# Later maskings, a later range check and another staging tile in a three-stage attention kernel

## The chip, the cores and the metric

The kernel runs on one core of one Trainium2 chip. The metric is the device time of one execution in microseconds (us). All runs compared here are of the fast state; executions of one kernel scatter: 45 of the kernel before, on one chip, lay between 2189.8 and 2222.5 us, with a median of 2202.0.

## The reference, cut to what matters

The output is a gated sum of two attention branches over 2048 tokens of width 640.

```
g = sigmoid((x * gate_w).sum(-1))
a = sliding-window attention, 32 heads of 20, window 256        # A_ref
b = recurrence over 64 segments of 32 tokens, each with 8       # B_ref
    memory tokens made from the segment before, 32 heads of 192
out = g * a + (1 - g) * b
```

## The kernel before

It has three stages. The **sliding branch** takes the tokens in 16 blocks of 128. The **tail** is named after the last 8 of each segment's 32 tokens: it computes their projections for all segments at once, before the recurrence. The **recurrent branch** follows, three quarters of the time.

In the sliding branch a group of scores goes through TensorE (scores), ScalarE (exponential) and VectorE (masking by a minimum), and its values are multiplied two groups later. Between these, "filling units" make the projections of the next block; they share two banks (tag "p") of PSUM, the memory that matmuls write to, and VectorE or ScalarE copies them out:

```python
def probs(qb, hf, u, pr):
    ...                                             # 8 score matmuls
    nc.scalar.activation(out=pt, in_=sp[:], func=ACT.Exp, scale=scale)
    ...
    nc.vector.tensor_tensor(out=pt, in0=pt, in1=pat..., op=ALU.min)      # the masking
...
for i, (hf, u, pr, done) in enumerate(units):
    (probs_exact if exact else probs)(qb, hf, u, pr)
    while fill and spent * total < (i + 1) * time:  # filling units
        w, f = fill.pop(0); f(); spent += w
    ready.append([(qb, hf, g, pr) for g in done])
    if len(ready) > 2:
        for v in ready.pop(0): values(*v)           # two groups later
if exact or qb == NB - 1 or len(chunks(qb + 1)) != nk:
    ...                                             # empties ready
```

The tail's loop, over four groups g of 24 units (eight banks "ps"):

```python
tail.qk(g, *u, tps, "ps")
if i == 11:
    tail.store_qk(g, 0)
    if g == 0:
        ... omg_sb memset and loads ...             # GpSimd
        step_c = step_constants(tc, bconst, chk)    # GpSimd; VectorE's mk_x inside
...
if g == 0 and i == 14:
    range_flag(tc, chk, tps, rl_all, flag)          # VectorE's check, then a count matmul
```

`step_constants` ends with `mk_x`, a VectorE reduction of `mk_h`, which GpSimd makes. The tail's query and key units are staged in two tiles, `holds[0]` for the first half of the segments, `holds[1]` for the second; the values that follow are staged in `holds[1]`.

## Time and profile before

In the lines of the profile PE is TensorE, PEld its weight loads, DVE VectorE, ACT ScalarE, POOL GpSimd, SP SyncE; L241 is line 241 of that run's kernel. A line of the order in time has start and duration in us, and in brackets the engine's idle time before it and what ended that. The granted clock is the share of full speed at which TensorE's clock ran.

| before | us |
|---|---|
| median of the first 3 runs | 2198.5 |
| profiled execution | 2206.7 |
| its sliding branch, to the store of the last gate column | 316.8 |
| its tail, to the first recurrent projection | 174.5 |
| its recurrent branch | 1715.4 |
| TensorE's granted clock, mean | 0.977 |

The stage marks are the start of the write of omg_dram (316.81 us) and of the first ps_k matmul (491.31 us). The lines of the waits and of the order in time stand in the prediction. The row of the page that shows the clock, in tenths of full speed over 40 slices of 55 us, before:

```profile
PEclk9998988999999999999999999999999999999999
```

The first two eights are in the sliding branch, the third (331 to 386 us) is in the tail. How it looks at 1 us, in a table of windows (busy time of PE, PEld, DVE, ACT and POOL, each with its number of instructions, then clock, DMA share and GB/s):

```profile
102.00:103.00 1.00, 0.67 (x19) 0.58 (x16) 0.62 (x2) 1.00 (x2) 0.00 (x0) 1.00 0.02 5
103.00:104.00 1.00, 0.21 (x4) 0.21 (x4) 1.00 (x3) 1.00 (x2) 0.00 (x0) 1.00 0.93 248
104.00:105.00 1.00, 1.00 (x26) 0.87 (x23) 0.97 (x4) 0.24 (x1) 0.13 (x1) 1.00 0.80 304
105.00:106.00 1.00, 1.00 (x18) 0.97 (x19) 1.00 (x2) 0.98 (x1) 1.00 (x4) 0.61 0.09 16
```

TensorE pauses for 1.1 us of two, and at 105 us its clock falls to half, for 13.7 us. Summed over such windows from 30 us to its end, the sliding branch loses 23.9 us of clock (one minus the granted clock, times time). That is no loss of run time as it stands: TensorE isn't the limit all the time.

### The profile page before, as it was taken

How to read it: one execution, taken by the hardware profiler on the slowest of the kernel's cores; microseconds unless marked ns; L12 is line 12 of the kernel's file. 1: busy time of each engine (PE TensorE's matmuls, PEld its weight loads, DVE VectorE, ACT ScalarE, POOL GpSimd, SP SyncE). 2: the span in 40 equal slices, each digit the busy share in tenths (PEclk: the TensorE clock that was granted, in tenths of full speed). 3: DMA queues.
4: the chain of work that ended last, by engine and by line, in shares of the span. 5: the costliest groups of instructions: out<-in, count | busy, mean ns of one | idle time of the engine just before them, and what ended most of it. 6: DMA issues, size and time to landing. Idle time of an engine off the chain costs nothing. (4 is left out here: it accounts for less than half of the span.)

```text
span 2206.7 us, 92693 instructions
## 1 busy us (share of the span) xinstructions
PE 1959.8 (89%) x39670; PEld 1455.9 (66%) x39670; DVE 1032.0 (47%) x3338; ACT 914.2 (41%) x1885; POOL 717.8 (33%) x2011
## 2 busy tenths in 40 slices
PE   7889988998988889989998898899988899898897
PEld 6777767756666666666666666666666666666665
DVE  5777753234444444444444444444444444444444
ACT  4766742233443434434433333344334343333343
POOL 4111102133333333333333333333333333333332
PEclk9998988999999999999999999999999999999999
DMA  4222119579999999999999999999999999999998
GB/s 140 75 69 71 43 26 320 140 213 344 362 352 346 340 349 355 360 347 348 364 347 336 351 356 342 342 356 360 348 344 356 354 356 350 362 337 355 336 352 287
DMA packets 278374, 655.81 MB, mean 297 GB/s; under 512 B 42552, under 2 KB 62144, under 8 KB 277952
## 3 DMA queue, kind: packets, MB, share of 16 engines
q1 hardware_dynamic: 246464, 602.01, 76.0%
q0 software_dynamic: 31488, 47.78, 7.5%
q8 instruction: 313, 5.13, 0.9%
q14 instruction: 109, 0.89, 0.1%
HBM read 620.26 MB, written 29.37 MB: 294 GB/s over the span
## 5 line engine op out<-in xcount | busy, mean ns | idle before, releaser
L763 PEld LDWEIGHTS <-b_hT 128*32 128x32 bf16 x15360 | 377.5, 96 | 311.4 <-issue 114.3
L954 PEld LDWEIGHTS <-b_OT 128*64 128x64 bf16 x6144 | 400.9, 110 | 67.2 <-issue 59.4
L954 PE MATMUL ps_o<-b_w,b_OT 128*64 128x320 bf16 x2560 | 300.4, 302 | 36.9 <-DMA b_w<-in_B_Wo_dram 33.0
L774 ACT CAST b_tok<-ps_k 128x384 bf16<-128x384 f32 x256 | 122.7, 479 | 441.3 <-PE ps_k L763 441.2
L763 PE MATMUL ps_k<-w_k,b_hT 128*32 128x384 bf16 x4096 | 246.8, 329 | 19.0 <-DVE b_hT L980 18.7
L954 PE MATMUL ps_o<-hold,b_OT 128*64 128x320 bf16 x2560 | 238.7, 302 | 0.0
L763 PE MATMUL ps_v<-w_v,b_hT 128*32 128x384 bf16 x3840 | 229.0, 328 | 7.2 <-issue 6.8
L763 PE MATMUL ps_q<-w_q,b_hT 128*32 128x384 bf16 x3840 | 235.2, 329 | 0.0
L239 ACT ACTIVATE pt<-s_ps 128x1024 bf16<-128x1024 f32 x180 | 180.7, 1024 | 75.3 <-PE s_ps L236 73.1
L934 ACT CAST b_OT<-ps_pv 128x480 bf16<-128x480 f32 x256 | 143.2, 559 | 164.7 <-PE ps_pv L930 114.0
L810 DVE COPY b_K<-tr_k 128x256 bf16<-128x256 bf16 x256 | 73.4, 287 | 291.3 <-PE tr_k L787 286.3
L774 ACT CAST b_vtok<-ps_v 128x384 bf16<-128x384 f32 x256 | 122.9, 480 | 168.2 <-PE ps_v L763 167.8
L963 DVE CAST b_osum<-ps_o 128x320 bf16<-128x320 f32 x64 | 31.5, 492 | 338.4 <-PE ps_o L954 338.4
L774 ACT CAST b_tok<-ps_q 128x384 bf16<-128x384 f32 x256 | 122.7, 479 | 112.5 <-PE ps_q L763 111.2
L716 POOL DMA_DIRECT2D b_xg<-xin x256 | 139.4, 545 | 84.9 <-POOL b_QT L800 57.0
L241 DVE TENSOR_TENSOR pt<-pt,pat 128x1024 bf16<-128x1024 bf16 x180 | 126.7, 708 | 69.6 <-ACT pt L239 69.4
L787 PEld LDWEIGHTS <-b_tok 128*64 128x64 bf16 x3072 | 100.6, 110 | 82.8 <-issue 33.5
L852 DVE TENSOR_REDUCE sm<-S_ps 128x4 f32<-128x160 f32 x256 | 82.1, 321 | 156.3 <-PE S_ps L841 149.1
L985 POOL DMA_DIRECT2D b_dram<-b_osum x128 | 64.2, 506 | 265.1 <-DVE b_osum L963 256.7
L986 POOL DMA_DIRECT2D b_ga<-ga_dram x128 | 63.5, 497 | 265.1 <-DMA out_dram<-b_ga 259.9
L907 DVE TENSOR_TENSOR b_PTm<-PT_ps,mk_m 128x320 bf16<-128x320 f32 x256 | 123.7, 483 | 49.2 <-PE PT_ps L895 47.2
L819 POOL COPY b_K<-b_xg 128x64 bf16<-128x64 bf16 x256 | 61.4, 240 | 258.8 <-PE S_ps L841 130.6
(142 smaller groups left out, 3832.4 us busy)
## 6 DMA issues: line engine op xcount, KB each, us to landing
b_w<-in_B_Wo_dram SPq DMA_DIRECT2D x640, 320.0 KB, 5.3
b_w<-in_B_Wq_dram SPq DMA_DIRECT2D x320, 384.0 KB, 5.6
b_w<-in_B_Wv_dram SPq DMA_DIRECT2D x320, 384.0 KB, 5.5
b_w<-in_B_Wk_dram SPq DMA_DIRECT2D x256, 384.0 KB, 5.7
xin<-hold POOLq DMA_DIRECT2D x8, 1536.0 KB, 9.7
b_xg<-xin POOLq DMA_DIRECT2D x256, 48.0 KB, 4.9
w_k<-in_B_Wk_dram SPq DMA_DIRECT2D x16, 384.0 KB, 3.3
b_xv<-xin POOLq DMA_DIRECT2D x64, 96.0 KB, 5.7
```

Of the source, the lines that this page charges most:

```text
L239: nc.scalar.activation(out=pt, in_=sp[:], func=ACT.Exp, scale=scale)
L241: nc.vector.tensor_tensor(out=pt, in0=pt, in1=pat.unsqueeze(1).to_broadcast([P, 2, 512]), op=ALU.min)
L716: sc.op("DMA", 500, lambda: nc.gpsimd.dma_start(tile_of(b)[:].rearrange("p i b t -> p (i b t)"), xin[s, :, c:c + 192]), writes=[b])
L763: nc.tensor.matmul(t[32 * j:32 * j + 32, 0:384], lhsT=tile_of(hT)[:, kt, :], rhs=w[:, j * 384:(j + 1) * 384], start=(kt == 0), stop=(kt == ...
L774: nc.scalar.copy(dst, src)
L787: nc.tensor.transpose(t[64 * a:64 * a + 64, k, :], tok["tile"][:, c:c + 64], ident[:], tile_position=(0, 64 * a))
L810: nc.vector.tensor_copy(tile_of(K02)[:, :, :, 0:SEG], src)
L852: nc.vector.tensor_reduce(out=x["mx"][:], in_=view(), axis=AX.X, op=ALU.max)
L907: nc.vector.tensor_tensor(out=tile_of(PTm)[:], in0=src.to_broadcast([P, 2, 4, L]), in1=mk_m[:].unsqueeze(1).unsqueeze(3).to_broadcast([P, ...
L934: sc.op("ACT", act(480), lambda: nc.scalar.copy(tile_of(OT)[:, 0:12 * L], o["tile"][:, 0:12 * L]), reads=[o], writes=[OT])
L954: nc.tensor.matmul(t[64 * h:64 * h + 64, 0:D // 2], lhsT=OT["tile"][:, c:c + 64], rhs=w, start=(g == 0 and m == 0 and n == 0), stop=(g == ...
L985: sc.op("DMA", 500, lambda h=h: nc.gpsimd.dma_start(half(b_dram, h), mine(osum["tile"], h)), reads=[osum])
```

## The change

Its intent: VectorE should not stand before an instruction that cannot start while others behind it could, and a staging tile should not be reused while its store is on the way. Nothing is computed differently.

```diff
-            nc.vector.tensor_tensor(out=pt, in0=pt, in1=pat..., op=ALU.min)
+            return lambda: nc.vector.tensor_tensor(out=pt, in0=pt, in1=pat..., op=ALU.min)
 ...
-                q0, q4, k4 = ([(140, lambda: dense.pop(0)(ps_p, "p"))] for _ in range(3))
+                q0, k0, q4 = ([(140, lambda: dense.pop(0)(ps_p, "p"))] for _ in range(3))
 ...
-                (probs_exact if exact else probs)(qb, hf, u, pr)
+                cut_next = (probs_exact if exact else probs)(qb, hf, u, pr)
+                if cut is not None:
+                    cut()
+                cut = cut_next
 ...
             if exact or qb == NB - 1 or len(chunks(qb + 1)) != nk:
+                if cut is not None:
+                    cut()
+                    cut = None
 ... tail: step_constants ahead of omg_sb, mk_x as c.last, the count as a function
-                    if g == 0 and i == 14:
-                        range_flag(tc, chk, tps, rl_all, flag)
+                    if g == 0 and i == 12:
+                        count = range_flag(tc, chk, rl_all, flag)
+                    if g == 1 and i == 0:
+                        step_c.last()
+                        count(tps, "ps")
 ... tail values
-        slot = self.holds[1][:, tt * PIECE:(tt + 1) * PIECE]...
+        slot = self.holds[0][:, tt * PIECE:(tt + 1) * PIECE]...
-                    if g == 0 and tt == 1:
+                    if g == 0 and tt == 3:
-                            weights.load_held(holds[0], i, u, nc.sync)
+                            weights.load_held(holds[1], i, u, nc.sync)
```

More of the change, by code (lines that the diff above doesn't have):

```diff
@@ L240, in probs @@
             pat = pats[nk][:].rearrange("p g c q -> p (g c) q")[:, 4 * u:4 * u + 4, :].rearrange("p i q -> p (i q)")
-            nc.vector.tensor_tensor(out=pt, in0=pt, in1=pat.unsqueeze(1).to_broadcast([P, 2, 512]), op=ALU.min)
+            return lambda: nc.vector.tensor_tensor(out=pt, in0=pt, in1=pat.unsqueeze(1).to_broadcast([P, 2, 512]), op=ALU.min)
         def probs_exact(qb, hf, u, pr):
@@ L300, in branch_A @@
         spread(1)
-        ready = []
+        ready, cut = [], None
         for qb in range(NB):
@@ L364, in mix, with range_flag @@
             nc.sync.dma_start(outf[rows, :], ga[:])
-def range_flag(tc, const, psum, rl_all, flag):
+def range_flag(tc, const, rl_all, flag):
     nc = tc.nc
@@ L378, in range_flag, with count @@
     nc.vector.memset(ones[:], 1.0)
-    n = psum.tile([1, 1], FP32, name="n_ok", tag="ps")
-    nc.tensor.matmul(n[:], lhsT=both[:], rhs=ones[:], start=True, stop=True)
-    nc.vector.tensor_scalar(out=flag[:], in0=n[:], scalar1=127.5, scalar2=None, op0=ALU.is_lt)
+    def count(psum, tag):
+        n = psum.tile([1, 1], FP32, name="n_ok", tag=tag)
+        nc.tensor.matmul(n[:], lhsT=both[:], rhs=ones[:], start=True, stop=True)
+        nc.vector.tensor_scalar(out=flag[:], in0=n[:], scalar1=127.5, scalar2=None, op0=ALU.is_lt)
+    return count
 L = MEM + SEG
@@ L586, in v @@
     def v(self, g, tt, pool, tag):
-        slot = self.holds[1][:, tt * PIECE:(tt + 1) * PIECE].rearrange("p (j c) -> p j c", j=4)
+        slot = self.holds[0][:, tt * PIECE:(tt + 1) * PIECE].rearrange("p (j c) -> p j c", j=4)
         xv = self.xin[:, :, KT * SEG + 768:XIN]
@@ L649, in step_constants @@
     mk_x = const.tile([P, 4], FP32, name="mk_x")
-    nc.vector.tensor_reduce(out=mk_x[:], in_=mk_h[:].rearrange("p g j -> p j g"), axis=AX.X, op=ALU.add)
     mk_z = const.tile([P, 2], FP32, name="mk_z")
@@ L656, in step_constants @@
     c = Constants()
+    c.last = lambda: nc.vector.tensor_reduce(out=mk_x[:], in_=mk_h[:].rearrange("p g j -> p j g"), axis=AX.X, op=ALU.add)
     c.still, c.ident, c.mask, c.mk_m, c.mk_x, c.mk_z = still, ident, mask, mk_m, mk_x, mk_z
@@ L1118 @@
                         if g == 0:
+                            step_c = step_constants(tc, bconst, chk)
                             nc.gpsimd.memset(omg_sb[:], 0.0)
@@ L1122 @@
                                     nc.gpsimd.dma_start(omg_sb[64 * h + MEM:64 * h + L, :], omg_dram[:].rearrange("(s t) -> t s", t=SEG))
-                            step_c = step_constants(tc, bconst, chk)
                         tail.fetch("q", g + 1)
                         tail.fetch("k", g + 1)
-                    if g == 0 and i == 14:
-                        range_flag(tc, chk, tps, rl_all, flag)
+                    if g == 0 and i == 12:
[3 more added lines that the diff above has]
+                        count(tps, "ps")
                         nc.gpsimd.dma_start(flag_dram[:], flag[:])
@@ L1140 @@
                     tail.v(g, tt, tps, "ps")
-                    if g == 0 and tt == 1:
+                    if g == 0 and tt == 3:
                         for i, u in enumerate(last[:HOLD]):
-                            weights.load_held(holds[0], i, u, nc.sync)
+                            weights.load_held(holds[1], i, u, nc.sync)
     with ExitStack() as bctx:
-        branch_B(bctx, tc, xin, mem0, weights, ring, step_c, omg_sb, ga_dram, b_dram, outf, holds[1], last[HOLD:])
+        branch_B(bctx, tc, xin, mem0, weights, ring, step_c, omg_sb, ga_dram, b_dram, outf, holds[0], last[HOLD:])
     wctx.close()
```

## The prediction

> **What bounds the kernel now.** I first read the table of busy shares (TensorE 89% of 2206.7 us, every other engine under 50%), then the slices in time, then tables of busy time over short windows, the list of waits of TensorE, and the instructions in order of time where it stood still. The program has three stages: the sliding branch to about 311 us, the tail (memory tokens' projections) to 490 us, the recurrent branch to the end. The change touches only the first two, so only TensorE's idle time and slow-clock time before 490 us can be won; the other 1717 us run the same instructions in the same order.
>
> The list of waits of TensorE, sliding branch without its start (30 to 311 us):
> ```profile
> PE qk_ps L138 <- DVE QT_blk L144: 11.9, 14, 1.0
> PE qk_ps L138 <- DVE KT_blk L144: 10.9, 13, 1.5
> PE s_ps L236 <- ACT pt L239: 3.1, 14, 0.5
> PE aT_ps L198 <- DVE an L291: 3.0, 2, 2.1
> PE o_ps L280 <- DVE pt L241: 1.1, 2, 0.6
> ```
> The columns are total us, times, longest us. Two waits a block of 128 tokens, near 0.9 us each, are for a projection bank that VectorE has not emptied: 22.8 us. The same list for the tail:
> ```profile
> PE n_ok L380 <- DVE ones L378: 14.6, 1, 14.6
> PE t_psv L593 <- ACT hold L559: 4.8, 1, 4.8
> PE t_psum L575 <- DVE hold L561: 1.7, 4, 0.9
> ```
> Two standstills. Why VectorE was late, from VectorE and GpSimd in order of time (start, duration, in brackets the idle time before):
> ```profile
> 337.34 0.18 DVE L650 TENSOR_REDUCE mk_x<-mk_h 128x4 f32<-128x16 f32 x1 [14.91 <-POOL mk_z L653]
> ...
> 330.89 0.99 POOL L624 MEMSET b_QT<- 128x504 bf16 x2
> ...
> 337.09 0.21 POOL L647 TENSOR_SCALAR_AFFINE_SELECT mk_h<-mk_h 128x16 f32<-128x16 f32 x1
> ```
> VectorE sits 14.9 us at the reduction for mk_x, whose input GpSimd finishes at 337.3 us; the range check stands behind it on VectorE, and TensorE's count matmul behind the check.
>
> And why the projection copy of the sliding branch is late, all engines in one block:
> ```profile
> 181.56 0.20 ACT L176 ACTIVATE ez<-zc 128x1 f32<-128x1 f32 x1 [1.10 <-DVE zc L174]
> 181.67 2.83 ACT L239 ACTIVATE pt<-s_ps 128x1024 bf16<-128x1024 f32 x3
> ...
> 182.71 0.69 DVE L241 TENSOR_TENSOR pt<-pt,pat 128x1024 bf16<-128x1024 bf16 x1 [0.37 <-ACT pt L239]
> ...
> 183.31 0.68 DVE L144 CAST QT_blk<-qk_ps 128x512 bf16<-128x512 f32 x1
> ...
> 184.05 0.72 PE L138 MATMUL qk_ps<-xT_blk,WkP 128*128 128x128 bf16 x10 [0.93 <-DVE QT_blk L144]
> ```
> The projection was complete at 181.2 us (its 20 matmuls start at 179.93 and take 1.29). VectorE was free at 182.33 but stood before a masking whose exponential had not ended, and did the copy only after it.
>
> **What the Trainium skill says.** "TensorE: Matmul & The Clock Gate", Architectural detail, calls ACT and DVE strict FIFO; the trace agrees: a ready copy waits 0.37 us behind an unready masking, and the range check 14.9 us behind mk_x. The same page, Part 1, says that the array clock falls to half after an idle window of about 3.4 us and needs about 3.4 us of work to come back. The tail agrees: after the 14.6 us gap fifteen matmuls start 0.21 us apart instead of 0.11 until 343.9 us; after the 4.8 us gap three units take 4.55 us (442.22 to 446.77) instead of 3 x 0.81. The page, HAM oscillation, speaks of whole idle windows, but here shorter pauses seem to be enough: in the 1 us windows of the sliding branch each of six half-clock stretches (from 105, 163, 238, 255, 276 and 296 us, lasting 3 to 14 us) starts right after such pauses. Before the first, TensorE is busy 0.67 and 0.21 us in the windows from 102 and 103 us, and the clock drops to 0.61 at 105. That part is my reading of coincidences.
>
> **The change part by part.**
>
> 1. *Masking one group later.* Nothing is added or removed: the 180 maskings (708 ns each) move behind the next group's exponential in program order. VectorE then meets a masking whose exponential ended about a group earlier (groups are 1.2 to 1.6 us apart), and the evacuations after it go when TensorE is done. In the block above the gate's copies would come near 179.6 instead of 181.1 us, so ScalarE's 1.1 us before ez falls too; the copy QT runs 181.2 to 181.9 and the next projection, due about 183.1, does not wait. A steady block now takes 17.77 us (VectorE's copies of xT_blk, 202.28, 220.05, 237.81); without 0.93 + 1.0 + 0.19 of waits it is 15.65. Twelve exponentials at 0.95 to 1.02 us and ScalarE's copies (0.58 + 0.57 + 0.20) make 12.7 to 13.6 us, VectorE's share of a block is about 13.5 (23 us in 30), so both fit, VectorE at 86%, and some waits will reappear. Values are multiplied two groups after their scores, so a masking one group late keeps about one group of slack. I take 80% of 22.8: **18 us**.
>
> 2. *Clock in the sliding branch.* The two blocks with a 13 us half-clock stretch take 22.3 and 22.4 us, 4.6 more than a clean one; the 10.7 us one costs about 3.6 in proportion, the three short ones 0.3 to 0.5 each (18.09 against 17.77 us): together near 14 us. If the pauses cause them, most go; if not, none. I take half: **7 us**.
>
> 3. *Dense units earlier in the last block.* A 2.07 us wait of the transposes for "an" at 295.7 us gets a unit of 10 matmuls (about 1.1 us at full clock) in front of it, as do the small waits after 311 us in part: **2 us**, and 1 for the half-clock stretch at 296.
>
> 4. *Count and mk_x later.* The check's vector work, 2.0 us, stays; it now comes after unit 12, and the count and mk_x twelve units of 1.09 us later, near 339.2 us on the old time axis. GpSimd's constants, started right after the store's issue at 325.4 instead of behind the 5.3 us of omg work, last 6.4 us before mk_h is complete (330.9 to 337.3), so they end near 332. Nobody waits. The gap of 14.6 goes, and the slow clock after it, 15 x 0.10 = 1.5: **16 us**.
>
> 5. *Tail values in the half stored first.* Its last store is issued at 419.0 instead of 432.1 us. At the 8.8 to 17.3 us that these stores take to land it is away by 436 at worst, in the median by 429, and the first copy is due at 431.6 with eight banks (6.5 us of values) before TensorE stops. The 4.8 us go, and the slow clock, 4.55 - 2.43 = 2.1: **7 us**. The held weights go to the other half after the fourth value tile (13 us into the values), when the late store of that half has landed.
>
> Sum: 18 + 7 + 3 + 16 + 7 = 51 us; 2198.5 - 51 = about **2147 us**, 2.3% faster.
>
> **The rivals.**
>
> *The DMA replaces the gap.* From 330 to 370 us the DMA share is 1.0, and with 15 us less in the tail the same weights are wanted earlier. For it: the second store of the tail was issued at 353.34 and held VectorE until 367.56, 14 us. Now its half is rewritten 13 us after the issue while the loads are thickest; if it lands after 17 us, copies wait 4 us. Against it: TensorE has eight banks, 8.7 us of units, before it stops; the third group's streamed weights, issued at 344 and here landing in 6.7 us, are due near 365. It would give back 0 to 5 us: 2147 to 2152.
>
> *The sliding branch is bound by ScalarE and VectorE after all.* With blocks near 15.7 us VectorE is 86% and ScalarE 84% busy in uneven bursts, and with two score banks a late masking now delays the values. For it: TensorE already waits 3.1 us for score banks. Against it: VectorE idled 69 us before maskings, waiting for exponentials, which is what the new order avoids. Half the gain of parts 1 and 2 lost makes 2160.
>
> *The clock does not care.* If half-clock stretches are as frequent after as before, part 2 is 0: 2154, just on the 2% line. If all go and the waits too, 2135.
>
> *Only the tail counts.* If the maskings' new order gives nothing: 2198.5 - 23 = 2175, 1% faster. The waits are so plainly behind maskings that I give this one in twenty.
>
> **Range and chances.** The tail's 23 us are nearly sure (give or take 3), the sliding branch's 28 are not (give or take 9), and the three runs of before spread over 11.7 us. Eight in ten: 2132 to 2164. Faster by over 2% means under 2154.5, or over 44 us gained; since the tail gives about 22, the sliding branch must give 22 of an expected 28: 0.72. Within 2%: 0.27. Slower: 0.01, since nothing is added.
>
> **What would show it.** Right: steady blocks near 16 us between copies of xT_blk, TensorE's waits for QT_blk and KT_blk under 6 us in all, the sliding branch ended near 283 us instead of 311, the granted clock there over 0.91; no TensorE wait over 1 us at n_ok or at the first t_psv, and the tail, from there to the first recurrent projection, about 23 us shorter; the recurrent branch as long as before to some us. Wrong: new waits of TensorE for values' maskings (o_ps or its weight load behind VectorE's pt), for a store's landing, or for weights in the tail; half-clock stretches as long as before without pauses ahead of them; or a recurrent branch that starts earlier and ends no earlier, its DMA share being 0.9 and more.

## The result, and the profile after

The changed kernel takes 2146.8 us (median of 4 runs, 2141.0 to 2152.6) against 2201.7 for the kernel before in the same rounds (4 runs). The ratio of the fast runs is 0.9755, with a 95% interval of 0.9712 to 0.9798: faster. A ratio here is the mean time of one kernel's fast runs over that of the other's in the same rounds, so not quite the ratio of the medians.

| profiled execution | before | after | difference |
|---|---|---|---|
| sliding branch, to the omg_dram store | 316.8 | 281.6 | -35.2 |
| tail, to the first recurrent projection | 174.5 | 151.9 | -22.6 |
| recurrent branch | 1715.4 | 1705.8 | -9.6 |
| whole | 2206.7 | 2139.3 | -67.4 |
| clock lost in the sliding branch from 30 us on | 23.9 | 5.1 | -18.8 |

The profiled execution of the changed kernel was its fastest run, so its difference, 67 us, is larger than that of the medians, 55. The last 9.6 us come from a stage whose instructions did not change; see the end of the experiments.

The list of waits of TensorE after, sliding branch (30 to 282 us) and then the tail (282 to 433 us); total us, times, longest:

```profile
PE o_ps L280 <- DVE pt L241: 4.7, 4, 2.1
PE qk_ps L138 <- DVE KT_blk L144: 3.3, 12, 0.5
PE t_psum L584 <- DVE hold L570: 0.8, 3, 0.4
```
```profile
PE t_psum L584 <- DVE hold L570: 0.9, 1, 0.9
PE tp L756 <- ACT hold L568: 0.7, 1, 0.7
PE t_psum L584 <- DMA w_ring<-in_B_Wq_dram: 0.5, 1, 0.5
```

The waits for QT_blk are gone, those for KT_blk are 0.3 us each instead of 0.8, and n_ok and t_psv are no longer in the list. One line grew: four waits for a masked tile, 4.7 us instead of 1.1. The weight loads ahead of these matmuls wait for masked tiles too, 8.7 us in 16 waits instead of 1.3 in two; this overlaps with the 4.7 us and in part with running matmuls. The block that the prediction read, in order of time after:

```profile
178.05 1.29 PE L138 MATMUL qk_ps<-xT_blk,WqP 128*128 128x128 bf16 x20
178.46 0.21 ACT L176 ACTIVATE ez<-zc 128x1 f32<-128x1 f32 x1
178.55 1.03 ACT L239 ACTIVATE pt<-s_ps 128x1024 bf16<-128x1024 f32 x1
...
179.16 0.68 DVE L241 TENSOR_TENSOR pt<-pt,pat 128x1024 bf16<-128x1024 bf16 x1
...
179.76 0.68 DVE L144 CAST QT_blk<-qk_ps 128x512 bf16<-128x512 f32 x1
...
180.92 0.73 PE L138 MATMUL qk_ps<-xT_blk,WkP 128*128 128x128 bf16 x10
```

No bracket of idle time stands behind any of the lines. The masking before the copy is an older one, so the copy starts 0.4 us after its matmuls end (178.05 + 1.29), where before it was 2.1 us (181.22 to 183.31), and the next projection starts without a wait. ScalarE's ez no longer waits either.

In the tail VectorE still stands still once, but TensorE does not:

```profile
307.61 0.75 DVE L570 CAST hold<-t_psum 128x256 bf16<-128x256 f32 x2 [7.30 <-DMA xin<-hold]
308.29 0.17 DVE L665 TENSOR_REDUCE mk_x<-mk_h 128x4 f32<-128x16 f32 x1
```

The first store of staged queries, issued at 288.5 us, lands 19 us later, while the resident weights are being loaded; the copy that reuses its tile waits for it 7.3 us. The eight banks take that up. GpSimd has finished mk_h at 300.6 us, so mk_x waits for nothing.

### The profile page after: what moved, and what is told of

It is laid out like the page before. It is cut to its first block, busy times and chain, and to the rows that moved or that the text cites. A ratio compares the mean times of both kernels' runs of the same rounds, so it can differ in the third digit from the quotient of the medians.

```text
span 2139.3 us, 92706 instructions
## 1 busy us (share of the span) xinstructions
PE 1943.8 (91%) x39670; PEld 1442.4 (67%) x39670; DVE 1027.0 (48%) x3338; ACT 914.1 (43%) x1885; POOL 717.9 (34%) x2011
## 5 line engine op out<-in xcount | busy, mean ns | idle before, releaser
L867 ACT ACTIVATE S_ps<-S_ps 128x160 f32<-128x160 f32 x256 | 74.5, 291 | 143.4 <-DVE S_ps L864 139.1
```

The source lines that it names most:

```text
L867: nc.scalar.activation(out=view(), in_=view(), func=ACT.Exp, scale=scale)
```

## The experiments

Ten kernels ran, all correct and all of the fast state, each against the kernel before in its own rounds.

### Each part alone

**e1_masks_only** has the four hunks of the masking, nothing else.

> The kernel before with the maskings one group later and nothing else. Theory: a masking at the head of VectorE's queue, waiting for its exponential, holds back ready projection copies; so TensorE's waits for QT_blk and KT_blk fall from 22.8 to under 6 us, a steady block takes about 16.1 us between copies of xT_blk, half-clock time in the sliding branch falls from about 47 to under 15 us, and the run takes 2165 to 2175 us (27 to 36 less). Rival A: only the clock matters and it is luck: blocks stay near 17.7 us and the run is within 10 us of before. Rival B: ScalarE and VectorE bind the branch, half of the gain: about 2185 us.

Measured: 2174.6 us against 2202.0, ratio 0.9881 (0.9847 to 0.9915). The waits of TensorE in the sliding branch fall from 30.8 to 10.4 us, those for QT_blk and KT_blk from 22.8 to 3.3; the clock lost falls from 23.9 to 8.5 us, and the branch ends at 286.0 us. A steady block takes 16.09 us. From VectorE in order of time, before and with later maskings alone:

```profile
126.57 0.49 DVE L74 COPY xT_blk<-xT_ps 128x640 bf16<-128x640 bf16 x1
144.35 0.48 DVE L74 COPY xT_blk<-xT_ps 128x640 bf16<-128x640 bf16 x1
```
```profile
199.00 0.48 DVE L74 COPY xT_blk<-xT_ps 128x640 bf16<-128x640 bf16 x1
215.09 0.48 DVE L74 COPY xT_blk<-xT_ps 128x640 bf16<-128x640 bf16 x1
```

17.78 us a block became 16.09. The theory holds, both rivals fall; only the half-clock time came out at 17.1 us, a little over the 15 expected. In this one part lies half of the gain.

**e2_dense_only** has the other order of filling units in the last block.

```diff
-                q0, q4, k4 = ([(140, ...
+                q0, k0, q4 = ([(140, ...
```

> Only the order of the filling units in the last block changes. Theory: the 2.07 us wait of the transposes for an goes and with it perhaps the 3.4 us half-clock stretch behind it: 1 to 4 us less than before. Rival: the unit moved forward leaves the same hole later on: no change of the end of the sliding branch (within 1 us).

Measured: 2197.5 us against 2202.0, ratio 0.9987 (0.9966 to 1.0009), so not told apart from nothing by the times. In the waits of TensorE those for the tile `an` fall from 3.0 us in two to 0.9 in one, which is what the theory said. I count it as 2 us shown by the trace and not by the time. The end of the branch, 308.7 us, lies 4 us before the earliest of five profiles of the old branch (312.8 to 318.7 us), which scatter by 6 us themselves, so it can't settle 2 us.

**e3_count_only** has the tail's constants, count and mk_x moved as in the change.

> Only the count, mk_x and the step constants move. Theory: the 14.6 us wait of n_ok goes with 1.5 us of slow clock behind it and nothing takes its place: 16 us less than before, tail shorter by 16. Rival: with the tail's loads packed closer, TensorE waits for streamed weights or for stores to land, and 5 us or more of it come back: at most 11 us less, with new waits by DMA in the tail.

Measured: 2181.9 us against 2202.0, ratio 0.9910 (0.9880 to 0.9939): 20 us by both, somewhat over the 16 expected. Its tail takes 157.7 us; those of the three profiles with the old tail (before, e1, e2) are 174.5, 175.1 and 177.2. So 17 to 20 us are from the tail. No wait by DMA of more than 2 us replaces n_ok.

**e4_slots_only** stages the tail values in the other half.

> Only the staging half of the tail values changes. Theory: the 4.8 us wait of the first values goes and 2.1 us of slow clock: 7 us less than before in the tail. Rival: the values' own stores, behind the big store in the same queue, land late, so the wait comes back at the second round of values or at the held weights: 0 to 3 us less.

Measured: 2194.6 us against 2202.0, ratio 0.9971 (0.9952 to 0.9989), 6.4 us by the ratio. The wait at t_psv, 4.8 us, is out of the list, and the tail takes 169.6 us, 5 to 8 less than with the old one. The product of the four ratios is 0.9751, and the whole change measured 0.9755: within the intervals the parts add up and do not hinder each other.

### Which instruction held the range check

**e5_mkx_only** moves mk_x alone, behind the count:

```diff
-    nc.vector.tensor_reduce(out=mk_x[:], in_=mk_h..., op=ALU.add)        # in step_constants
+    c.last = lambda: nc.vector.tensor_reduce(out=mk_x[:], in_=mk_h..., op=ALU.add)
 ...
+                    if g == 1 and i == 0:
+                        step_c.last()
```

> The kernel before with mk_x's reduction moved behind the count, at the second group's first unit; constants, check and count stay where they were. Theory: mk_x at the head of VectorE's queue is the cause; without it the check runs at once, n_ok waits 1 to 3 us (the check's 2.0 us of vector work and a copy stand before it) instead of 14.6 to 15.5, the run takes 13 to 16 us less than before. Rival: the check's own work or the count in TensorE's order is the cause: n_ok still waits over 8 us.

**e6_n_ok_only** leaves mk_x ahead of the check and moves the count and the flag to the same place.

> The kernel before with the count alone moved to the second group's first unit; mk_x's reduction stays ahead of the check. Theory: VectorE still stands about 14.9 us for GpSimd's constants, and TensorE runs on until its eight banks are full, 6 to 8 units of 1.09 us, then waits 4 to 8 us at t_psum: 6 to 11 us less than before. Rival: the count alone is the cause, VectorE's stand is hidden: 14 to 17 us less and no TensorE wait over 1 us.

Measured: 2188.4 us, ratio 0.9929 (0.9908 to 0.9951), and 2188.6 us, ratio 0.9933 (0.9909 to 0.9958). The two lines of n_ok in the waits of TensorE, of e5 (line 380) and of e6 (line 382):

```profile
PE n_ok L380 <- DVE ones L378: 2.4, 1, 2.4
```
```profile
PE n_ok L382 <- DVE ones L378: 4.4, 1, 4.4
```

With mk_x out of the way the wait is 2.4 us, the check's own work and a copy, as expected. With mk_x in the way and the count later, TensorE goes on to 333.4 us and then waits 4.4 us. So mk_x at the head of VectorE's queue is the cause, and TensorE's place of the count sets how much of VectorE's stand is seen. I had e6 wrong in two things: the wait is at n_ok, which comes due before the banks run out, and the gain is 15 us by the ratio (9 to 20 by its interval) where I expected 6 to 11; its tail is 10.4 us shorter than the one before. By the run times the two can't be ranked; both keep most of the gain, and the change's combination of them takes the rest (tails of 160.8 and 164.1 us against 157.7).

### How late a masking may be

**e7_two_later** puts the maskings two groups later:

```diff
+                if len(cuts) == 2:
+                    cuts.pop(0)()
+                if cut is not None:
+                    cuts.append(cut)
```

> The changed kernel with the maskings two groups later instead of one. Theory: a masking then has no slack left before the values that need it: TensorE waits for masked tiles (o_ps or its weight load behind pt) 10 to 40 us in all, and the run is that much longer than the changed kernel (2157 to 2187 us). Rival: anything that keeps the masking from the head of the queue is as good: within 4 us of the changed kernel.

Measured: 2176.4 us against 2203.0, ratio 0.9879, so some 30 us slower than the changed kernel, whose ratio is 0.9755. The sliding branch ends at 314.1 us. The wait line that grew:

```profile
PE o_ps L280 <- DVE pt L241: 23.5, 38, 2.3
```

The theory holds. The values stand two groups after the scores; one group of delay uses slack, a second uses it up.

### Whether pauses bring the half clock

The changed kernel has two long waits for a masked tile, at 31 and 48 us, where the number of key blocks changes and the loop empties its pending maskings and values. Both are followed by half-clock stretches. **e8_no_flush** takes the emptying away there:

```diff
-            if exact or qb == NB - 1 or len(chunks(qb + 1)) != nk:
+            if exact or qb == NB - 1:
```

> The changed kernel without the emptying of the pending maskings and values where the number of key blocks changes (after the first and second blocks). Theory: the waits of 2.15 and 1.52 us for a masked tile at 31 and 48 us go, and because such pauses bring the half clock, the half-clock stretches at 32 and 49 us go as well: 4 to 7 us less than the changed kernel. Rival on the clock: half-clock stretches come by themselves; as many as in the changed kernel (2 to 4), 2 to 4 us less.

Measured: 2135.5 us against 2203.0, ratio 0.9700 (0.9654 to 0.9746). Windows of the changed kernel, then of e8 (us, TensorE busy first, the clock third from the end):

```profile
30.00:32.00 2.00, 0.23 (x8) 0.23 (x8) 1.61 (x6) 0.00 (x0) 0.00 (x0) 1.00 0.00 0
32.00:34.00 2.00, 2.00 (x28) 1.77 (x25) 0.75 (x2) 1.02 (x1) 0.00 (x0) 0.52 0.00 0
```
```profile
30.00:32.00 2.00, 2.00 (x50) 1.85 (x46) 1.46 (x8) 1.50 (x3) 0.00 (x0) 1.00 0.01 5
32.00:34.00 2.00, 1.53 (x33) 1.29 (x30) 2.00 (x5) 1.02 (x1) 0.00 (x0) 1.00 0.06 17
```

In e8 one half-clock stretch is left in the sliding branch from 30 us on, from 259.8 to 263.2 us in the last block, where TensorE was busy only 0.50 us from 258 to 259 us; the changed kernel had three, at 32, 49 and 264 us. The two behind the emptying are gone, the one in the last block, which did not change, stays. The branch ends 4.4 us earlier (277.2 us), as expected, and the rival falls. The whole is 11 us faster by the medians; the difference over 4.4 us isn't in the changed stage, and the two kernels were timed in different calls, so I leave it to scatter.

**e9_four_pauses** puts the pauses back at other places, into e8:

```diff
-            if exact or qb == NB - 1:
+            if exact or qb in (4, 7, 10, 13) or qb == NB - 1:
```

> The kernel without the flush at changes of block size (e8), but with the pending maskings and values emptied after blocks 4, 7, 10 and 13, which makes TensorE wait for a masked tile there. Theory on the clock: a pause of 1.5 to 2 us within a few us brings the half clock: half-clock stretches begin within 4 us of at least three of the four pauses where e8 has none, and the run takes 10 to 20 us more than e8 (2145 to 2156 us). Rival: stretches come by themselves: none or one near the pauses, and only the pauses' own 4 to 8 us more (2139 to 2144 us).

Measured: 2159.6 us against 2203.1, ratio 0.9800, 24 us more than e8 by the medians. The four pauses in order of time, from TensorE:

```profile
94.36 0.44 PE L280 MATMUL o_ps<-V_blk,pt 128*128 128x21 bf16 x10 [1.47 <-DVE pt L241]
150.41 0.41 PE L280 MATMUL o_ps<-V_blk,pt 128*128 128x21 bf16 x10 [1.47 <-DVE pt L241]
204.05 0.42 PE L280 MATMUL o_ps<-V_blk,pt 128*128 128x21 bf16 x10 [1.47 <-DVE pt L241]
253.68 0.42 PE L280 MATMUL o_ps<-V_blk,pt 128*128 128x21 bf16 x10 [1.47 <-DVE pt L241]
```

Windows of 2 us, one behind each pause (the clock third from the end):

```profile
95.00:97.00 2.00, 2.00 (x25) 1.80 (x20) 0.58 (x2) 1.02 (x1) 0.00 (x0) 0.50 0.00 0
153.00:155.00 2.00, 2.00 (x26) 1.41 (x23) 2.00 (x4) 1.39 (x2) 0.22 (x1) 0.50 0.03 8
205.00:207.00 2.00, 2.00 (x40) 1.61 (x37) 1.23 (x3) 1.47 (x2) 0.00 (x0) 1.00 0.03 8
255.00:257.00 2.00, 2.00 (x24) 1.80 (x23) 0.13 (x1) 0.64 (x1) 0.00 (x0) 0.50 0.00 0
```

Half-clock stretches run from 93.7 to 110.8, from 151.7 to 162.0 and from 254.1 to 257.5 us, behind the first, second and fourth pause; behind the third there is none. So "at least three of four" came true and the rival's "none or one" missed; the run time is a little over the 2145 to 2156 us expected. e8 has no stretch in these blocks. So pauses can bring the half clock. Other profiles agree: the six with the masking at its old place lose 17.1 to 30.7 us of clock in this branch, the four with it one group later and no pause put in (the changed kernel, e1, e8, e10) 0 to 8.5.

The sliding branch is 15.8 us longer than in e8 (293.0 against 277.2): the pauses themselves are 6 us, and the other 10 us go with 13.7 us more of clock lost (15.4 against 1.7).

Why the third pause of the same 1.47 us brought nothing stays open. In the clock records of all twelve profiles a half-clock stretch lasts 1 to 5 times 3.41 us, and in one profile all of them start on one grid of that step. But how busy TensorE was in the step before does not settle it: before the six stretches of the kernel before it was 37 to 74%, and in e9 67% in the step from 202.9 us, which holds most of the third pause, with no stretch behind it.

### A version that beats both

**e10_kt_on_scalar** is e8 with all key projections copied by ScalarE:

```diff
-                    if isq or g < 4:
+                    if isq:
                         nc.vector.tensor_copy(dst, pst[:])
```

> e8 with all copies of KT_blk on ScalarE instead of half of them. Theory: VectorE is the fuller of the two in a block, and TensorE's last regular wait there is for its copy of KT_blk (3.9 us in 13): that wait goes and 2 to 5 us with it (about 2132 us). Rival: 0.58 us more a block on ScalarE, which does all exponentials, delays scores: TensorE waits for s_ps or masked tiles instead, same time or up to 6 us more than e8.

Measured: 2127.1 us against 2203.1, ratio 0.9668 (0.9633 to 0.9702), the fastest of all kernels here. The waits of TensorE in its sliding branch (30 to 268 us):

```profile
PE o_ps L280 <- DVE pt L241: 1.1, 2, 0.6
PE qk_ps L138 <- ACT KT_blk L146: 0.7, 1, 0.7
PE t_psum L584 <- DVE hold L570: 0.6, 2, 0.4
PE qk_ps L138 <- DVE QT_blk L144: 0.5, 1, 0.5
```

That is 2.9 us in all, and no half-clock stretch is left there. A steady block takes 15.68 us (108.61 to 124.28 us between copies of xT_blk), and the branch ends at 268.9 us, 8.4 us before e8, and by the medians the run is 8 us faster, where I had expected 2 to 5. ScalarE is busy 138.6 us of the 160 from 100 to 260 us, VectorE 133.9, and neither makes TensorE wait over 0.7 us at once.

### The recurrent branch

It has the same instructions in all twelve profiles, and took from 1700.7 us (e10) to 1728.6 us (e2). In them TensorE's waits for streamed weights vary from 69 to 85 us and the clock lost there from 7 to 23 us. In the profiled pair these waits are 85.1 and 75.5 us, which is the whole of the 9.6 us. The six profiles with the values staged in the other half have 1706.6 us in the mean, the other six 1714.6; but e4, which makes just this change, gained 2.4 to 10.6 us in all by its interval, and its tail alone accounts for 5 to 8. So I take the 9.6 us for scatter of this stage; why the weights come later in one execution than in another stays open.

## Why the prediction was right

The time was foretold as 2147 and came out as 2146.8 us. That is closer than its parts.

1. *Maskings, 18 us.* Right, and slightly small: with later maskings alone the two waits that it named fell by 19.5 us, all of TensorE's waits in the branch by 20.4. The mechanism, a copy held behind an unready masking in a strict queue, is shown by e1 from one side and by e7 from the other. The block came to 16.09 us between the 15.65 without any wait and the 17.77 of before.
2. *Clock, 7 us.* Right in direction, and too small: it took half of an estimate of 14 us. The clock lost fell by 18.8 us, by 15.4 with the maskings alone. The branch became 35.2 us shorter, of which 22.0 are waits of TensorE (30.8 against 8.8); the other 13 us are near the whole 14, though this remainder was not measured by itself. What the prediction called a reading of coincidences is supported by e8, e9 and e10: without pauses no stretch in the steady blocks, with four pauses three. Which pause does it was not settled.
3. *Last block, 3 us.* The wait of 2.07 us went (e2); the time itself is within scatter.
4. *Count and mk_x, 16 us.* Right: 17 to 20 us of tail in e3. The rival of the DMA was real in part: the store took 19 us and VectorE stood 7.3 us for it. It cost TensorE nothing, for the reason given, eight banks.
5. *Staging tile, 7 us.* Right: 6.4 us by the ratio of e4.

The sum of the first three, 28 us, was too small by 7 against the 35.2 of the branch in the profiles, which is about what the clock was taken too small by; the tail's 23 met 22.6. (The prediction ends the branch at about 311 us, some 6 us before the mark of the tables, so only differences can be compared, not its 283 with 281.6.) The profiled pair differs by 67 us in part because the recurrent branch was lucky in it; the medians differ by 55, the point estimate said 51 to 52. The remaining 3 or 4 us are less than the scatter of four runs (11.6 us), and part of the agreement to a fraction of a microsecond is luck: the baseline, too, moved from 2198.5 to 2201.7.

One of its signs of being wrong, new waits for the values' maskings, came true in a small way (4.7 us), and one of its signs of being right says little: a granted clock over 0.91 in the branch, which had 0.92 before and has 0.98 after.

The place of these waits it did not name: where the block size changes, the change empties the pending masking just before the values that need it. TensorE then waits 2.1 and 1.5 us, with slow clock behind it. That makes most of the line that grew, and e8 removes these two waits.

## What to carry to other kernels

In a strict queue an instruction that waits costs everything behind it that is ready: place it where its input is already there, but no later than its own reader allows, and look for that reader's slack first (one group here gained 27 us, two groups gave it back: e7 ends the branch at 314.1 us). Where a loop is emptied at a boundary, the deferred work loses its slack just there. A short wait of TensorE can cost more than its length, because the clock may fall behind it (6 us of pauses made the branch of e9 15.8 us longer), so look at the granted clock next to the waits.

## What the Trainium skill lacked or had wrong

- "TensorE: Matmul & The Clock Gate", Why this matters for your kernels, asks for "No PE-idle gaps >~3µs between matmul bursts". Here the clock fell to half behind pauses of 1.5 to 2.2 us (the changed kernel at 31 and 48 us; e9, three of four pauses of 1.47 us) and behind 1.1 us of idle time within two (before, 102 to 104 us). The section on PSUM-queue cycling of the same page does say that frequent short idles can make the clock swing, which the prediction overlooked; it gives no length of a pause.
- The same page, Part 1, gives about 3.4 us of work for the clock to come back. That held in the tail (3.2 us of slow matmuls after the gap), but in the sliding branch some half-clock stretches lasted 10 to 17 us with TensorE nearly always busy (93.7 to 110.8 us in e9: 81% in the first 3.41 us, then 100%). No run here shows why.
- The same page, Architectural detail, calls ScalarE and VectorE strict FIFO, which these runs confirm. No page that I read draws the conclusion for the order of instructions: here it was worth 14.9 us of VectorE's idle time at one reduction, and 27 us of the run for the place of 180 maskings.
